# Loading one row of a weight as 85, 30 and 13 partitions instead of 128

## The chip, the cores and the metric

The kernel runs on one core of a Trainium2 chip. The metric is device time in microseconds (us); lower is better. A load is carried in packets by the 16 DMA engines that the page counts. The semaphore of a load of 128 partitions gets 16 increments in these traces; I read one increment as one engine's part landed, and the load as landed with the last of them.

A ratio below is the mean time of one kernel's fast runs over the mean of the other's in the same rounds, so it is not quite the ratio of the medians that stand beside it.

## The reference

One token (S = 1, D = 1024) goes through two branches that are added: grouped attention over a cache of 65,536 keys (4 groups of 8 heads, 128 wide), and an MLP. What matters here is how the sum ends:

```python
x = A_x
xn = _layernorm(x, axis=-1)
return x + _A_ref(xn, k_cache, v_cache, wq, wo) + _B_ref(xn, w1, w2, w3, w4)
# in _B_ref:  h2 = _gelu(_layernorm(x1) @ w3) @ w4      w4 is 3584 x 1024, bf16
```

Nearly all of the time goes into reading 170 MB of caches and weights once.

## The kernel before

All caches and weights are loaded in one stream on SyncE's queue, in the order in which it is used, through three big buffers. The weight w4 comes last, in eight pieces. Partition m holds rows 28m to 28m+27 of w4; "a row of the tile" below is one of these 28 for all 128 partitions, 2 KB a partition. A piece of n rows is n times 2 KB for each of 128 partitions.

```python
W4_PIECES = (6, 5, 6, 4, 3, 2, 1, 1)
# ... (cut)
    stream.append("w4")                      # the last item of the stream
# ... (cut)
            elif it == "w4":
                w4_v = B_w4.rearrange("(m c) n -> m c n", c=FC)
                c0 = 0
                for n in W4_PIECES:
                    go(out=t[:, c0 * D:(c0 + n) * D], in_=w4_v[:, c0:c0 + n, :].rearrange("p c n -> p (c n)"))
                    c0 += n
# ... (cut)
    def compute_w4(lo, hi):                  # two matmuls for each of the 28 rows, in order
        wt = st.tiles["w4"]
        for c in range(lo, hi):
            for j in range(2):
                row_acc(j, hT[:, c:c + 1], wt[:, D * c + 512 * j:D * c + 512 * (j + 1)])
# ... (cut)
    compute_w4(early, FC)
    out_t = ogpool.tile([64, 512], BF16, name="out_t", tag="og")
    nc.scalar.copy(out=out_t[:], in_=psB[0:64, :])
    nc.scalar.dma_start(out=out[0, 0, :].rearrange("(j n) -> j n", j=2), in_=...)   # cut
```

## Time and profile before

| | before |
|---|---|
| time, median of 3 runs (us) | 401.73 (401.62 to 401.75) |
| span of the profiled run (us) | 399.7 |
| TensorE / VectorE busy | 57% / 52% |
| DMA: share of 16 engines, rate | 98.7%, 425 GB/s |
| last w4 piece landed (us) | 394.90 to 396.90, by engine |

Three lines of the page of before: all DMA packets, then the queue of the load stream (packets, MB, share of 16 engines' span) and the queue of instruction fetches.

```profile
DMA packets 4575, 170.01 MB, mean 425 GB/s; under 512 B 467, under 2 KB 469, under 8 KB 982
...
q1 hardware_dynamic: 4560, 169.87, 98.7%
q8 instruction: 8, 0.13, 0.1%
...
```

The stream keeps the DMA engines busy for 98.7% of the span, so the kernel is bound by DMA. The eight packets of queue 8 are fetches of instructions, 16 KB each.

The chain of waits of before, its last stretch (start us, us, what):

```profile
337.53 41.96 DMA big<-in_A_v_cache_dram
...
379.51 17.39 DMA big<-in_B_w_dram
...
396.94 0.40 PE psB L221 x2
...
397.36 0.58 ACT out_t L485
```

The V load hands over to the w4 load, w4 lands at 396.90 us, and behind it are only two matmuls and the cast. The store follows. What moves the last landing moves the end.

SyncE's line of the timeline of before (start, us, what): all eight pieces are issued, the last after a wait of 14.5 us for a semaphore that the V load still used (its last increment came at 379.49 us; the last piece counts on the same one).

```profile
361.80 18.04 SPq L183 DMA_DIRECT2D big<-in_B_w_dram  x8
```

The trace also lists each increment of a load's semaphore. The sixteen of the last piece of before, in us:

```
394.90 394.96 394.96 394.99 395.06 395.11 395.26 | 396.06 | 396.51 396.54 396.55 396.60 396.66 396.76 396.81 396.90
```

Seven engines are early, one is in the middle and eight are late. The landings of the earlier loads show why. After each of the eight instruction fetches (0.94 to 1.10 us a packet, at 43.3, 106.2, 156.8, 200.3, 255.9, 297.1, 336.1 and 383.4 us) one more engine is late, by about 1.6 us, and stays so to the end; after a smaller fetch (8 KB, at 113.4 us) one more is late by about 1.1 us, the one in the middle. So each fetch went through another engine, by these counts. The engines do not catch up: a 2 KB packet takes 84 ns (median; 96 at most), early or late.

### The profile page before, as it was taken

How to read it: one execution, taken by the hardware profiler on the slowest of the kernel's cores; microseconds unless marked ns; L12 is line 12 of the kernel's file. 1: busy time of each engine (PE TensorE's matmuls, PEld its weight loads, DVE VectorE, ACT ScalarE, POOL GpSimd, SP SyncE). 2: the span in 40 equal slices, each digit the busy share in tenths (PEclk: the TensorE clock that was granted, in tenths of full speed). 3: DMA queues.
4: the chain of work that ended last, by engine and by line, in shares of the span. 5: the costliest groups of instructions: out<-in, count | busy, mean ns of one | idle time of the engine just before them, and what ended most of it. 6: DMA issues, size and time to landing. Idle time of an engine off the chain costs nothing.

```text
span 399.7 us, 2547 instructions
## 1 busy us (share of the span) xinstructions
PE 229.8 (57%) x1348; PEld 44.8 (11%) x854; DVE 209.0 (52%) x154; ACT 27.3 (7%) x35; POOL 5.4 (1%) x28
## 2 busy tenths in 40 slices
PE   0561960591579247832964296429453936494985
PEld 0210000000200110010101000201010002010241
DVE  0610010975196559644953795269349931985040
ACT  1001010003000200020002000200100020002000
POOL 2000000000000000000000000000000000000000
PEclk9996895697769587968895679679976986597999
DMA  9998999999999999999999999999999999999995
GB/s 420 420 448 384 436 485 439 426 420 420 415 427 426 446 472 421 426 420 426 433 428 466 439 420 426 415 446 426 446 448 426 420 426 402 430 469 426 397 421 227
DMA packets 4575, 170.01 MB, mean 425 GB/s; under 512 B 467, under 2 KB 469, under 8 KB 982
## 3 DMA queue, kind: packets, MB, share of 16 engines
q1 hardware_dynamic: 4560, 169.87, 98.7%
q8 instruction: 8, 0.13, 0.1%
q14 instruction: 1, 0.01, 0.0%
q10 hardware_dynamic: 6, 0.00, 0.0%
HBM read 169.87 MB, written 0.00 MB: 425 GB/s over the span
## 4 chain that ended last, share of the span: by engine, by line
DMA 52%; DVE 26%; PE 16%; ACT 3%; another core or an unknown queue 2%; issue 1%; DVEq 0%; ACTq 0%
DMA big<-in_A_k_cache_dram 31%; DVE big L357 19%; DMA big<-in_A_v_cache_dram 10%; PE sc L362 8%; PE oacc L412 6%; DMA big<-in_A_wq_dram 5%; DMA big<-in_B_w_dram 4%; DVE p_sb L383 3%; DVE mx L367 3%; ACT p_sb L380 3%; PE psq L287 1%; PE pm_mx L369 0%; DVE m L371 0%; PE pm_mx L376 0%
## 5 line engine op out<-in xcount | busy, mean ns | idle before, releaser
L362 PE MATMUL sc<-big,qdiag 128*128 128x512 bf16 x512 | 129.0, 413 | 66.8 <-DVE big L357 61.2
L357 DVE STREAM_TRANSPOSE big<-big 128x4096 f32<-128x4096 f32 x32 | 139.4, 4412 | 50.5 <-DMA big<-in_A_k_cache_dram 50.5
L412 PE MATMUL oacc<-big,p_sb 128*32 128x512 bf16 x512 | 43.0, 509 | 34.5 <-DVE p_sb L383 34.5
L367 DVE TENSOR_REDUCE mx<-sc 128x1 f32<-128x2048 f32 x8 | 18.3, 2292 | 29.8 <-PE sc L362 29.8
L362 PEld LDWEIGHTS <-qdiag 128*128 128x128 bf16 x128 | 13.2, 103 | 178.1 <-issue 145.8
L380 ACT ACTIVATE p_sb<-sc,nball 128x2048 bf16<-128x2048 f32 x8 | 15.7, 1967 | 220.6 <-DVE nball L378 220.6
L383 DVE STREAM_TRANSPOSE p_sb<-p_sb 128x2048 bf16<-128x2048 bf16 x8 | 18.5, 2312 | 18.0 <-ACT p_sb L380 18.0
L412 PEld LDWEIGHTS <-p_sb 128*32 128x32 bf16 x512 | 17.2, 124 | 57.4 <-DVE p_sb L383 35.1
L287 PE MATMUL psh<-big,ln_rep_b 128*32 128x512 bf16 (+1 forms) x64 | 12.4, 943 | 8.3 <-DMA big<-in_B_w_dram 8.3
L451 PE MATMUL o_acc<-big,oT 128*1 128x512 bf16 x48 | 12.0, 415 | 2.4 <-ACT p_sb L380 2.4
L369 PE MATMUL pm_mx<-ident_f,mx 128*1 128x128 f32 x8 | 2.4, 296 | 19.1 <-DVE mx L367 19.1
L326 DVE STREAM_TRANSPOSE h_row<-h_row 128x896 bf16<-128x896 bf16 x1 | 1.1, 1111 | 21.4 <-ACT h_row L325 21.4
L421 DVE SCALAR_TENSOR_TENSOR og<-oacc,wb,og 128x512 f32<-128x512 f32 x4 | 3.0, 746 | 16.2 <-PE oacc L412 16.2
L221 PE MATMUL psB<-big,hT 128*1 128x512 bf16 x56 | 7.4, 378 | 2.2 <-DMA big<-in_B_w_dram 2.1
L457 DVE COPY o_rows<-o_acc 1x1024 f32<-1x1024 f32 x1 | 1.2, 1212 | 12.8 <-PE oacc L412 12.8
L235 PE MATMUL pm_ln<-ln_rowsum_a,ones_f 128*128 128x1 f32 x2 | 0.6, 348 | 12.6 <-DVE ln_rowsum_a L233 12.6
L311 POOL COPY qdiag<-qx 32x32 bf16<-32x32 bf16 x16 | 3.3, 204 | 279.4 <-PE sc L362 250.3
L433 PE MATMUL pm_e<-ol,sel8big 128*128 128x129 f32 x8 | 2.3, 370 | 8.2 <-DVE ol L432 8.2
L226 DVE STREAM_TRANSPOSE x_t<-x_row 32x256 bf16<-32x256 bf16 x4 | 2.5, 616 | 8.2 <-DMA x_row<-in_A_x_dram 8.1
L287 PE MATMUL psq<-big,ln_rep_a 128*32 128x512 bf16 x64 | 5.6, 527 | 1.2 <-DMA big<-in_A_wq_dram 1.2
L376 PE MATMUL pm_mx<-ident_f,rep 1*128 1x1 f32 x8 | 1.8, 228 | 5.0 <-DVE rep L373 5.0
L299 DVE CAST q_row<-psq 128x512 bf16<-128x512 f32 x1 | 0.7, 692 | 7.5 <-PE psq L287 7.5
(95 smaller groups left out, 72.4 us busy)
## 6 DMA issues: line engine op xcount, KB each, us to landing
big<-in_A_wo_dram SPq DMA_DIRECT2D x1, 8192.0 KB, 37.2
big<-in_B_w_dram SPq DMA_DIRECT2D x1, 7168.0 KB, 38.2
big<-in_B_w_dram SPq DMA_DIRECT2D x2, 2048.0 KB, 46.4
big<-in_B_w_dram SPq DMA_DIRECT2D x2, 1536.0 KB, 27.3
big<-in_B_w_dram SPq DMA_DIRECT2D x1, 1280.0 KB, 24.1
big<-in_B_w_dram SPq DMA_DIRECT2D x1, 1024.0 KB
big<-in_B_w_dram SPq DMA_DIRECT2D x1, 768.0 KB, 30.8
big<-in_B_w_dram SPq DMA_DIRECT2D x1, 512.0 KB, 31.5
```

The source lines that it names most:

```text
L221: nc.tensor.matmul(psB[32 * j:32 * j + lhsT.shape[1], :], lhsT=lhsT, rhs=rhs, start=start, stop=False, tile_position=(0, 32 * j), skip_gro ...
L226: nc.vector.transpose(out=x_t[32 * a:32 * a + 32].rearrange("p c j -> p (c j)"), in_=x_row[:, 256 * a:256 * (a + 1)].rearrange("p (i c) -> ...
L287: nc.tensor.matmul(acc[32 * q:32 * q + 32, i, 0:n], lhsT=rep[:, c, :], rhs=cols(c, i, q), start=(c == 0), stop=(c == DC - 1), tile_positio ...
L311: nc.gpsimd.tensor_copy(out=qdiag[at, LEAD:].rearrange("p (x c) -> p x c", x=4)[:, :, 32 * a:32 * a + 8], in_=qx[at, :, 8 * g:8 * g + 8])
L357: nc.vector.transpose(out=words, in_=words)
L362: nc.tensor.matmul(sc[:, e, :], lhsT=qdiag[:, c0:c0 + P], rhs=cols[:, s, e, :, b2, :, r], start=(s == 0 and b2 == 0 and r == 0), stop=(s = ...
L367: nc.vector.reduce_max(out=mx[:], in_=sc[:].rearrange("p e n -> p (e n)"), axis=AX.X)
L380: nc.scalar.activation(out=p_sb[:], in_=sc[:], func=ACTF.Exp, bias=nball[:, b:b + 1], scale=SCALE, accum_out=group["lall"][:, b:b + 1])
L383: nc.vector.transpose(out=flat, in_=flat)
L412: nc.tensor.matmul(oacc[32 * q:32 * (q + 1), :], lhsT=pT[:, e, 32 * t:32 * (t + 1)], rhs=vt[:, :, e, t, :], start=(e == 0 and t < 4), stop ...
L421: nc.vector.scalar_tensor_tensor(out=og[:], in0=oacc[:], scalar=wb[:, 1:2], in1=og[:], op0=ALU.mult, op1=ALU.add)
L451: nc.tensor.matmul(tail["rows"][0:1, h2, :], lhsT=oT[g][:, j:j + 1], rhs=wt[:, g, j, 512 * h2:512 * (h2 + 1)], start=(g == 0 and j == 0), ...
```

## The change

The intent is to even this out: one row of the tile is not loaded over 128 partitions, 8 for each engine, but as 85, 30 and 13 partitions. The semaphores of these three loads get 5, 15 and 13 increments from DMA engines, instead of 16. If each load is dealt evenly, one of the five engines of the 85 partitions carries 17 to 20 rows, any other at most 3. The five are meant to be early engines, which take work from the late ones; that they are early was assumed.

```diff
-W4_PIECES = (6, 5, 6, 4, 3, 2, 1, 1)
+W4_PIECES = (6, 5, 6, 3, 1, 3, 2, 1, 1)
+W4_SHARED = 4
+SHARES = (85, 30, 13)
...
-                for n in W4_PIECES:
+                for i, n in enumerate(W4_PIECES):
+                    if i == W4_SHARED:
+                        p0 = 0
+                        for k in SHARES:
+                            go(out=t[p0:p0 + k, c0 * D:(c0 + n) * D],
+                               in_=w4_v[p0:p0 + k, c0:c0 + n, :].rearrange("p c n -> p (c n)"))
+                            p0 += k
+                        c0 += n
+                        continue
```

## The prediction

> What bounds the kernel. DMA. The page's queue table has the load queue's packets busy for 98.7% of 16 engines' span, 425 GB/s; TensorE is busy 57%, VectorE 52%. In the chain of waits the V load ends at 379.49 us, then the w4 load runs 17.39 us to 396.90, then two matmuls (0.40), the cast (0.58) and the store. So the landing of the last w4 piece sets the end.
>
> By the trace's DMA packet and landing records this piece lands unevenly: seven of sixteen engines at 394.90 to 395.26 us, one at 396.06, eight at 396.51 to 396.90. The lag is older: eight 16 KB instruction fetches (queue 8, about 1.06 us each) went each through one engine and left it about 1.7 us behind for good. [...] A 2 KB packet takes 80 ns from start to start; late engines do not speed up when the early ones are done.
>
> What the change does. [...] Before, each engine carried 8 rows of this row of w4. [...] The bytes are the same. Three more DMA issues (about 0.43 us each) on SyncE wait for recycled semaphores; the last waits for the third piece (landed 389.97) and starts 1.2 us later, some 2 us before the queues run dry: hidden, by estimate.
>
> How much is critical. If an engine's own rate is the only limit, the late group ends 0.4 us earlier (396.5), the early five at 394.65+0.5+0.96=396.1: 401.3. [...] One engine here moves 65,536 B in 2.414 us, 27.1 GB/s[...]. [...] No line of this trace tells which limit holds. [...]predict no gain: 401.9 us, range 401.2 to 403.2. Chances: faster by over 2% 0.005, within 2% 0.98, slower by over 2% 0.015.
>
> What would show it. Last w4 landing at 396.5 with a narrower spread if only engine rates count; 396.9 or later, with the 85-partition load's 2 KB packets longer than 84 ns[...]. Matmuls, cast and store behind it unchanged, everything before 379 us too. SyncE issues the last piece at about 390 us.
>
> What would make it wrong. [...] A last issue so late that engines idle. Instruction fetches that move.

The sum weighed two branches. If only an engine's own rate counts, five engines, supposed early and with 12 rows more each (0.96 us at 80 ns a row), end at 396.1 us and the late ones with 5 rows fewer (0.4 us) at 396.5 us, which gave 401.3 us. In the other branch, to which 60% were given, rows that other engines carry collide where they are written, and nothing is gained. Together they came to 401.9 us. One of the risks: that the five engines are not all early, put at up to 1 us.

## More of the kernel before

Stretches of the end of before. The columns are the stretch, its length, the busy time and count of PE, PEld, DVE, ACT and POOL, the granted TensorE clock, the busy share of the 16 DMA engines, and GB/s:

```profile
core 0: us, PE busy (x) PEld busy (x) DVE busy (x) ACT busy (x) POOL busy (x), PEclk, DMA share, GB/s
387.00:389.00 2.00, 1.98 (x18) 0.95 (x20) 0.94 (x4) 0.00 (x0) 0.00 (x0) 1.00 0.99 416
389.70:390.70 1.00, 1.00 (x14) 0.37 (x10) 0.00 (x0) 0.00 (x0) 0.00 (x0) 1.00 1.03 428
390.70:391.70 1.00, 1.00 (x12) 0.41 (x9) 0.00 (x0) 0.00 (x0) 0.00 (x0) 1.00 0.99 410
391.70:392.70 1.00, 0.42 (x6) 0.09 (x3) 0.00 (x0) 0.00 (x0) 0.00 (x0) 1.00 0.99 404
392.70:393.70 1.00, 0.83 (x8) 0.26 (x5) 0.00 (x0) 0.00 (x0) 0.00 (x0) 1.00 0.99 395
393.70:394.70 1.00, 0.32 (x4) 0.17 (x5) 0.00 (x0) 0.00 (x0) 0.00 (x0) 1.00 0.93 361
```

The DMA share stays near 1.00 and the rate near 400 to 430 GB/s until engines run out of work.

## The result, and the profile after

| | before | after |
|---|---|---|
| time, median of 6 runs (us) | 401.62 (401.40 to 401.75) | 403.27 (403.03 to 403.55) |
| span of the profiled run (us) | 399.7 | 401.3 |
| last w4 piece landed (us) | 394.90 to 396.90 | 396.01 to 398.28 |

The ratio is 1.0041 (95% interval 1.0028 to 1.0054): slower by 1.65 us, outside the predicted range by 0.07 us and far from its centre.

The same lines of the page of after:

```profile
DMA packets 4736, 170.01 MB, mean 424 GB/s; under 512 B 500, under 2 KB 502, under 8 KB 1271
...
q1 hardware_dynamic: 4721, 169.87, 98.7%
q8 instruction: 8, 0.13, 0.1%
...
```

The bytes and the share of the queue are the same, with 161 packets more. The page as a whole hides what happened.

The chain of waits of after, its last stretch:

```profile
338.16 41.31 DMA big<-in_A_v_cache_dram
...
379.49 16.24 DMA big<-in_B_w_dram
...
395.77 3.17 PE psB L231 x14
...
398.96 0.58 ACT out_t L495
```

The chain names a piece that landed at 395.73 us and fourteen matmuls that ran without a gap after it. The last two of these still had to wait for the last piece, and that landed at 398.28 us, 1.38 us later than before. (Why there was no gap is told at the end of this section.)

SyncE's lines of the timeline of after: three loads of the shared row at 363.97 us, and the last four pieces from 379.49 on.

```profile
362.17 1.75 SPq L193 DMA_DIRECT2D big<-in_B_w_dram  x4
363.97 1.16 SPq L188 DMA_DIRECT2D big<-in_B_w_dram  x3
379.49 10.90 SPq L193 DMA_DIRECT2D big<-in_B_w_dram  x4
```

The last issue is at 390.06 us, as predicted, and its data land 6 to 8 us later, behind the queue. Issue is not what is late.

The stretches of after:

```profile
core 0: us, PE busy (x) PEld busy (x) DVE busy (x) ACT busy (x) POOL busy (x), PEclk, DMA share, GB/s
387.00:389.00 2.00, 1.74 (x16) 0.73 (x14) 1.38 (x5) 0.00 (x0) 0.00 (x0) 1.00 1.00 418
389.70:390.70 1.00, 1.00 (x12) 0.43 (x10) 0.00 (x0) 0.00 (x0) 0.00 (x0) 1.00 1.01 260
390.70:391.70 1.00, 1.00 (x14) 0.37 (x10) 0.00 (x0) 0.00 (x0) 0.00 (x0) 1.00 1.08 272
391.70:392.70 1.00, 0.79 (x8) 0.23 (x5) 0.00 (x0) 0.00 (x0) 0.00 (x0) 1.00 1.01 268
392.70:393.70 1.00, 0.65 (x6) 0.17 (x5) 0.00 (x0) 0.00 (x0) 0.00 (x0) 1.00 0.98 324
393.70:394.70 1.00, 0.54 (x4) 0.12 (x3) 0.00 (x0) 0.00 (x0) 0.00 (x0) 1.00 0.98 393
```

This is the main reading. The early engines reach the shared row at 389.2 us, and from 389.7 us the 16 DMA engines are as busy as before (1.01, 1.08, 1.01), but they move 260, 272 and 268 GB/s instead of 428, 410 and 404. Busy share counts the time that packets are under way, so packets that take longer look busy.

The packet records say the same by packet. Between 389.9 and 392.9 us all 96 packets of 6 KB took 321 ns or more (median 359; in e1_pieces below, with the same pieces, 239.5), and all 89 of 2 KB took 98 ns or more (median 133; 84 there). No packet was spared, not even the 6 KB ones, which belong to loads of 128 partitions. The window is chosen to hold the stall: the first packets of the shared row, from 389.18 us, still took 84 to 92 ns; the slowing sets in for 2 KB and 6 KB packets alike between 389.6 and 389.8 us, and it is over at 393.8 us.

The landings by engine of the pieces that matter, in us:

```
85 partitions (5 engines):   391.80 392.06 392.12 392.15 | 393.77
last piece (16 engines):     396.01 396.03 396.14 | 397.07 397.13 397.14 397.20 397.22 397.25 397.30 397.33 397.43 397.52 397.65 397.72 | 398.28
```

Two things stand out. Thirteen of the sixteen engines end later than the latest engine of before (396.90), twelve of them by 0.2 to 0.8 us, although eleven engines were given fewer rows (at most 3 of the shared row, not 8, if the loads are dealt evenly). And one engine ends 0.56 us after all the others; by its lag it is one of the five with 17 rows or more, whose part of the 85 partitions landed 1.6 us after the other four. Only three of the seven early engines of before are still early in the last piece, so four of the five chosen engines were early ones, and the fifth was not. (The records carry no engine numbers; this is inferred from the counts.)

A small third part shows in the profiled run: from the last landing to the end of the cast it took 1.26 us (398.28 to 399.54) instead of 1.04 (396.90 to 397.94). Stretches of after at its end:

```profile
396.00:397.00 1.00, 1.00 (x6) 0.26 (x3) 0.00 (x0) 0.00 (x0) 0.00 (x0) 0.50 0.69 260
397.00:398.00 1.00, 1.00 (x8) 0.44 (x6) 0.00 (x0) 0.00 (x0) 0.00 (x0) 0.50 0.08 31
398.00:398.90 0.90, 0.90 (x6) 0.08 (x1) 0.00 (x0) 0.00 (x0) 0.00 (x0) 0.50 0.00 0
```

The granted TensorE clock was 0.50 there, and the matmuls fell behind and ran back to back. In the profiled run this is 0.22 of the 1.6 us by which the span grew; the other runs of after have no trace, so what it is worth in them is not known. It is not the main cause: the clock was 1.00 in the same place in the profiles of e2_even and e3_four below, which lose 1.44 and 1.55 us.

### The profile page after: what moved, and what is told of

The parts are those of the page before. It is cut to its first block, busy times and chain, and to the rows that moved or that the text cites. A ratio compares the mean times of both kernels' runs of the same rounds, so it can differ in the third digit from the quotient of the medians.

```text
span 401.3 us, 2551 instructions
## 1 busy us (share of the span) xinstructions
PE 233.7 (58%) x1348; PEld 44.6 (11%) x854; DVE 209.0 (52%) x154; ACT 27.3 (7%) x35; POOL 5.3 (1%) x28
## 4 chain that ended last, share of the span: by engine, by line
DMA 51%; DVE 26%; PE 17%; ACT 3%; another core or an unknown queue 2%; issue 1%; DVEq 0%; ACTq 0%
DMA big<-in_A_k_cache_dram 31%; DVE big L367 18%; DMA big<-in_A_v_cache_dram 10%; PE sc L372 8%; PE oacc L422 6%; DMA big<-in_A_wq_dram 5%; DMA big<-in_B_w_dram 4%; DVE p_sb L393 3%; DVE mx L377 3%; ACT p_sb L390 3%; PE psq L297 2%; PE psB L231 1%; DVE m L381 0%; PE pm_mx L379 0%
## 5 line engine op out<-in xcount | busy, mean ns | idle before, releaser
L422 PE MATMUL oacc<-big,p_sb 128*32 128x512 bf16 x512 | 45.4, 526 | 34.5 <-DVE p_sb L393 34.5
L231 PE MATMUL psB<-big,hT 128*1 128x512 bf16 x56 | 8.5, 438 | 2.1 <-DMA big<-in_B_w_dram 2.1
```

Source lines behind the costliest of these rows:

```text
L231: nc.tensor.matmul(psB[32 * j:32 * j + lhsT.shape[1], :], lhsT=lhsT, rhs=rhs, start=start, stop=False, tile_position=(0, 32 * j), skip_gro ...
L422: nc.tensor.matmul(oacc[32 * q:32 * (q + 1), :], lhsT=pT[:, e, 32 * t:32 * (t + 1)], rhs=vt[:, :, e, t, :], start=(e == 0 and t < 4), stop ...
```

## The experiments

Three theories were to be told apart. C: rows that are handed to other engines collide where they are written, and this slows the loads. U: the uneven counts are the loss, because an engine that already lags got more rows. P: the extra pieces, small packets and recycled semaphores cost time. Later a fourth came up, H: the rows are read from HBM in a worse order. Times that stand without their condition in the expectations of e7_comb and e8_alone2 are those for theory C. Counts of engines are known from increments: 16 for 128 partitions, 5 for 85, 4 for 68, 3 for 51, 15 for 30, 13 for 13. No count was taken for 80, 64 and 48 partitions, multiples of 16 as 128 is; 16 engines for these is my estimate from the counts above. Ten kernels ran in three jobs, on three chips; all gave correct results. The medians of before in the three jobs were 401.64, 401.65 and 401.57 us.

### e1_pieces: the pieces without the sharing

```diff
 # before.py
-W4_PIECES = (6, 5, 6, 4, 3, 2, 1, 1)
+W4_PIECES = (6, 5, 6, 3, 1, 3, 2, 1, 1)
```

> The pieces of the change (6, 5, 6, 3, 1, 3, 2, 1, 1), but every one a load of 128 partitions: no sharing. Theory C[...] and theory U (the five engines carry too many rows): neither is present, so the time of before, 401.5 to 401.8 us, last w4 landing about 396.9 us. Rival P (one more piece, smaller packets, waits of SyncE for recycled semaphores): most of the loss stays, 402.5 to 403.3 us.

Measured: 401.64 us (401.62 to 401.68), ratio 1.0001 (0.9986 to 1.0016). Two stretches of it:

```profile
389.70:390.70 1.00, 1.00 (x12) 0.43 (x10) 0.00 (x0) 0.00 (x0) 0.00 (x0) 1.00 1.07 432
...
391.70:392.70 1.00, 1.00 (x12) 0.38 (x10) 0.00 (x0) 0.00 (x0) 0.00 (x0) 1.00 1.03 418
```

The rate is that of before, and the last piece landed at 396.76 us. P falls: neither the ninth piece nor its issue costs anything that can be seen. (The change has two issues more than this kernel; e7_comb, with one more, shows no loss clear of the noise either.)

### e2_even: other rows, equal counts by estimate

```diff
 # after.py
-SHARES = (85, 30, 13)
+SHARES = (80, 48)
```

> The shared row as loads of 80 and 48 partitions[...]. Theory C: slow packets (2 KB well over 84 ns) around 390 to 393 us on all engines, last landing 397.3 to 398.3 us, 402.2 to 403.2 us in all. Theory U (uneven counts are the whole loss): as before, 401.5 to 401.9 us.

Measured: 403.08 us (402.75 to 403.25), ratio 1.0037 (1.0020 to 1.0054); last landing 398.04 us. Three stretches of it:

```profile
389.70:390.70 1.00, 1.00 (x12) 0.44 (x10) 0.00 (x0) 0.00 (x0) 0.00 (x0) 1.00 1.05 274
390.70:391.70 1.00, 1.00 (x12) 0.35 (x7) 0.00 (x0) 0.00 (x0) 0.00 (x0) 1.00 1.03 336
391.70:392.70 1.00, 0.11 (x2) 0.00 (x0) 0.00 (x0) 0.00 (x0) 0.00 (x0) 1.00 1.08 244
```

By the estimate above each engine has 5 + 3 = 8 rows of this row of the tile, as before, and most of the loss is there. If so, U as the whole cause falls. The same stall is seen: full DMA share at 244 to 336 GB/s.

### e3_four: four engines instead of five

```diff
 # after.py
-SHARES = (85, 30, 13)
+SHARES = (68, 60)
```

> 68 and 60 partitions[...]. Under both theories the load on the writers is about that of the change. [...]the 68-partition load has no straggler and the end comes near that of the other engines, 402.5 to 402.9 us; [...]403.2 to 403.7 us.

The first time is for the case that the straggler of the change (393.77 us against 391.80 to 392.15) is not among the four engines of the 68 partitions, the second for the case that it is.

Measured: 403.19 us (403.07 to 404.37), ratio 1.0046 (1.0031 to 1.0061). The 68 partitions landed at 391.90, 391.91, 392.38 and 393.71 us, and four engines instead of three were early in the last piece. So the straggler is still among the chosen ones (393.71 us).

### e4_alone: single loads by themselves

```diff
 # before.py, after the last matmul
+    for n in (128, 85, 80, 64, 30, 16, 13, 5, 128):
+        nc.sync.dma_start(out=w4_t[0:n, 0:8 * D], in_=w4_all[0:n, 0:8, :].rearrange("p c n -> p (c n)"))
```

Each load overwrites the one before it, so each waits until that one has landed: its first packet starts 0.94 to 1.36 us after the last landing of the one before (seven gaps).

> The kernel before, and after its last matmul nine loads of w4, one at a time, 16 KB a partition (605 ns a packet in the main stream), of 128, 85, 80, 64, 30, 16, 13, 5 and 128 partitions. If only an engine's own rate counts, the packets of each take rows per engine times 0.6 us: 4.8, 10.3, 3.0, 2.4, 1.2, 0.6, 0.6, 0.6, 4.8. [...] Total time about 450 us; results correct.

Measured (one look; first packet to last landing): 85 partitions 17.43 us, 80: 6.88, 64: 6.35, 30: 3.61, 16: 3.17, 13: 3.01, 5: 3.02, the last 128: 6.34. The first 128 overlapped with the stream and is left out. A load of 64 partitions takes as long as one of 128 (6.35 and 6.34 us) with half the rows; if both have 16 engines (an estimate), 4 rows an engine against 8, engine rates alone do not explain that. A load of 5 takes about as long as one of 16; with one row an engine in both (an estimate, as 13 partitions got 13 increments), this fits either theory. (e9_alone3 below settles it.) These times hold the landing too, and the expectation was of the packets alone. The 85 partitions need 17.43 us where 17 rows at 0.61 us, the time of a 16 KB packet in the stream, would be 10.4: the five engines are slowed even alone. In the small loads it is the landing that is late (16 partitions: packets done after 2.06 us, landed after 3.17).

### e5_dose: three rows of the tile shared instead of one

```diff
 # after.py
-W4_SHARED = 4
+W4_SHARED = 3
-SHARES = (85, 30, 13)
+SHARES = (80, 48)
```

> As e2_even (80 and 48 partitions[...]), but the piece that is shared is the one of three rows of w4 instead of one. Theory C, loss by collisions[...]: about three times the 1.44 us of e2_even, 404.8 to 406.2 us. Rival (a cost per load that is not of 128 partitions, whatever its size): as e2_even, 402.9 to 403.4 us.

Measured: 404.89 us (404.75 to 405.04), ratio 1.0080 (1.0065 to 1.0095). Two stretches of it:

```profile
389.70:390.70 1.00, 1.00 (x12) 0.35 (x10) 0.55 (x2) 0.00 (x0) 0.00 (x0) 0.97 0.85 176
...
391.70:392.70 1.00, 1.00 (x12) 0.35 (x10) 0.00 (x0) 0.00 (x0) 0.00 (x0) 1.00 1.08 188
```

The loss grows with the bytes: 3.24 us (404.89 less 401.65) against 1.44 (403.08 less 401.64), 2.25 times for three times the bytes. It is no fixed cost of a load with few partitions. It also is not quite proportional.

### e6_halves and e7_comb: neighbours against every other partition

```diff
 # after.py: e6_halves
-SHARES = (85, 30, 13)
+SHARES = (64, 64)
```

```diff
 # after.py: e7_comb
-SHARES = (85, 30, 13)
+SHARES = (0, 1)
-                            go(out=t[p0:p0 + k, c0 * D:(c0 + n) * D],
-                               in_=w4_v[p0:p0 + k, c0:c0 + n, :].rearrange("p c n -> p (c n)"))
-                            p0 += k
+                            go(out=t[k::2, c0 * D:(c0 + n) * D],
+                               in_=w4_v[k::2, c0:c0 + n, :].rearrange("p c n -> p (c n)"))
```

> The shared row as partitions 0 to 63 and 64 to 127[...]. Theory C: [...]slower than before by 0.6 to 1.6 us, 402.2 to 403.3 us. Theory U (uneven counts alone): 401.5 to 401.9 us.

> The same two loads of 64 partitions[...], but of the even and of the odd partitions[...]. [...]nearer to before, 401.6 to 402.4 us[...]. If it comes from loads of fewer than 128 partitions as such: as e6_halves.

Measured: e6_halves 402.78 us (402.61 to 403.08), ratio 1.0028 (1.0011 to 1.0044); e7_comb 401.85 us (401.67 to 401.88), ratio 1.0003 (0.9988 to 1.0018). Stretches of e6_halves, then of e7_comb:

```profile
389.70:390.70 1.00, 1.00 (x12) 0.37 (x10) 0.00 (x0) 0.00 (x0) 0.00 (x0) 1.00 1.09 303
390.70:391.70 1.00, 1.00 (x12) 0.44 (x10) 0.00 (x0) 0.00 (x0) 0.00 (x0) 1.00 1.00 328
391.70:392.70 1.00, 0.91 (x10) 0.26 (x5) 0.00 (x0) 0.00 (x0) 0.00 (x0) 1.00 1.12 291
```

```profile
389.70:390.70 1.00, 1.00 (x12) 0.44 (x10) 0.00 (x0) 0.00 (x0) 0.00 (x0) 1.00 1.07 430
390.70:391.70 1.00, 0.98 (x12) 0.30 (x8) 0.00 (x0) 0.00 (x0) 0.00 (x0) 1.00 1.01 404
391.70:392.70 1.00, 1.00 (x8) 0.22 (x8) 0.00 (x0) 0.00 (x0) 0.00 (x0) 1.00 1.02 414
```

The two differ in nothing but which 64 partitions make a load. With neighbours the rate falls to 291 to 328 GB/s; with every other partition it stays at 404 to 430 GB/s, the packets stay at 84 ns for 2 KB, and the loss is gone within the noise. So it is not the number of partitions of a load that costs, but where its partitions lie.

### e8_alone2: neighbours against spread partitions, alone

```diff
 # before.py, after the last matmul
+    for n, step in ((16, 1), (128, 8), (32, 1), (128, 4), (64, 1), (128, 2), (128, 1)):
+        nc.sync.dma_start(out=w4_t[0:n:step, 0:8 * D], in_=w4_all[0:n:step, 0:8, :].rearrange("p c n -> p (c n)"))
```

> The kernel before, then single loads alone, 16 KB a partition: 16 neighbouring partitions, 16 partitions 8 apart, 32 neighbours, 32 that are 4 apart, 64 neighbours, 64 that are 2 apart, 128. [...] first packet to last landing about 3.2 and 1.9, 3.2 and 1.9, 6.3 and 3.9, 6.3 us. If only engine rates count: within each pair the same, about 1.9, 1.9, 3.9 us and less.

Measured (one look): 16 partitions 8 apart 2.08 us; 32 neighbours 3.70, 32 that are 4 apart 2.45; 64 neighbours 6.28, 64 that are 2 apart 3.83; 128: 6.49. The first load overlapped with the stream and says nothing; 3.17 us of e4_alone stands for it. In each pair the spread partitions take less. From 32 to 64 neighbours the time nearly doubles (3.70 to 6.28 us), and from 64 to 128 it stays (6.49): the second 32 partitions behave as if they shared a limit with the first 32, the other 64 as if they had their own. The loads of 32 took 0.5 us longer than I had expected.

### e9_alone3: destination or source

In e6, e7 and e8 the partitions written and the rows read change together, so H was still open: 64 neighbours also read neighbouring stretches of w4. Here the two are set apart.

```diff
 # before.py, after the last matmul
+    for n, ds, ss in ((128, 1, 1), (64, 1, 1), (64, 1, 2), (64, 2, 1), (64, 2, 2), (16, 1, 8), (16, 8, 1), (5, 1, 1), (5, 4, 4)):
+        nc.sync.dma_start(out=w4_t[0:n * ds:ds, 20 * D:28 * D],
+                          in_=w4_all[0:n * ss:ss, 20:28, :].rearrange("p c n -> p (c n)"))
```

> The kernel before, then single loads alone, 16 KB a partition, after the last matmul (the tile is dead by then, so the results stay correct): 128 rows as a start; 64 rows with destination / source neighbouring or 2 apart in all four combinations; 16 rows to 16 neighbours from rows 8 apart and the reverse; 5 rows to 5 neighbours, and to 5 partitions that are 4 apart. [...]the destination alone decides: 6.3, 6.3 (neighbours) and 3.9, 3.9 us (2 apart), 3.2 and 2.1 us for 16 rows, 3.0 and about 1.6 to 1.9 us for 5 rows. If it sits in reading the rows (rival H), the source alone decides: 6.3, 3.9, 6.3, 3.9.

Measured (one look), as stretches from the first packet of each load to its last landing; the second column is its duration, the last its rate. In order: 64 rows to neighbours from neighbours, to neighbours from every other, to every other from neighbours, to every other from every other; 16 rows to neighbours, 16 rows to partitions 8 apart; 5 rows to neighbours, 5 rows to partitions 4 apart.

```profile
405.58:412.07 6.49, 0.00 (x0) 0.00 (x0) 0.00 (x0) 0.00 (x0) 0.00 (x0) 0.50 0.74 162
413.34:419.35 6.01, 0.00 (x0) 0.00 (x0) 0.00 (x0) 0.00 (x0) 0.00 (x0) 0.50 0.80 174
420.64:424.46 3.82, 0.00 (x0) 0.00 (x0) 0.00 (x0) 0.00 (x0) 0.00 (x0) 0.50 0.76 275
425.75:429.51 3.76, 0.00 (x0) 0.00 (x0) 0.00 (x0) 0.00 (x0) 0.00 (x0) 0.50 0.76 275
430.49:433.58 3.09, 0.00 (x0) 0.00 (x0) 0.00 (x0) 0.00 (x0) 0.00 (x0) 0.50 0.41 85
434.92:436.87 1.95, 0.00 (x0) 0.00 (x0) 0.00 (x0) 0.00 (x0) 0.00 (x0) 0.50 0.45 134
437.78:440.52 2.74, 0.00 (x0) 0.00 (x0) 0.00 (x0) 0.00 (x0) 0.00 (x0) 0.50 0.12 30
442.10:443.50 1.40, 0.00 (x0) 0.00 (x0) 0.00 (x0) 0.00 (x0) 0.00 (x0) 0.50 0.21 59
```

The destination decides: 6.49 and 6.01 us to neighbours, 3.82 and 3.76 us to every other partition, whatever is read. H falls for loads by themselves; in the stream no run sets the two apart. The last two lines are the plainest: five rows need 2.74 us to neighbours, and 1.40 us to partitions 4 apart (from rows 4 apart; I had expected 1.6 to 1.9).

### e10_three: three engines with 17 rows or more

```diff
 # after.py
-SHARES = (85, 30, 13)
+SHARES = (51, 77)
```

> 51 and 77 partitions[...]. Theory C alone[...]: as e2_even to e3_four, 402.9 to 403.4 us. If the load of the most loaded engine adds to it: [...]403.5 to 404.2 us[...]; [...]the time falls to 402.5 to 403.0 us.

The last time, 402.5 to 403.0 us, is for the case that the engine that lags by 1.2 us is not among the three; the one before it is for the case that it is.

Measured: 402.77 us (402.69 to 402.94), ratio 1.0030 (1.0013 to 1.0047). The 51 partitions landed at 392.27, 392.47 and 392.49 us: no straggler, with as many rows an engine of this load as in the change (51 on 3 and 85 on 5, 17 each if dealt evenly). The chain of waits of e10_three, its end:

```profile
386.01 11.87 DMA big<-in_B_w_dram
...
397.92 0.40 PE psB L231 x2
```

The last landing is at 397.88 us. By these landings the straggler is among the five of the change and the four of e3_four, and not among the three here (taken as one engine, an inference). Being rid of it is worth 0.50 us (403.27 less 402.77, from different jobs with the same time of before), which fits the 0.56 us by which it trailed in the change. (By the last landings alone it is 0.40 us, 398.28 less 397.88; the rest may be the slower clock at the end of the profile of after, and the rows are also dealt otherwise.) Three engines with 17 rows or more each cost no more than e2_even, whose counts are even by the estimate above (402.77 against 403.08 us), so uneven counts of early engines do not set the end.

## Why the prediction was wrong, point by point

- The bound was right. DMA sets the end and the last w4 landing moves it. What comes before is as it was: the V load ahead of the tail landed at 379.47 us, against 379.49.
- The number of engines was right: the semaphores of the three loads got 5, 15 and 13 increments from DMA engines, and one entry each within 0.6 us of the issue (364.47, 364.89, 365.30 us), of which the trace does not tell the writer. Which engines they are, no run here shows.
- The hidden issues were right: the last at 390.06 us, and neither e1_pieces nor e7_comb shows a loss clear of the noise. Matmuls and cast behind the last landing were not quite unchanged: 1.26 us instead of 1.04 in the profiled run.
- The branch on which I put 60%, collisions where the rows are written, was right. What I had said would show it came: a last landing after 396.9 (398.28 us) and 2 KB packets longer than 84 ns (133 in the median). e6_halves, e7_comb and e9_alone3 show the cause: with the same number of partitions and bytes, the partitions that are written decide (6.49 and 6.01 us to neighbours, 3.82 and 3.76 us to every other partition). So the other branch, a gain of 0.4 us if only engine rates count, is not what the runs show: 64 neighbours take about as long as 128 partitions (6.28 and 6.49 us in e8_alone2).
- The step that failed is the cost of the collisions, in its reach and in its size. My text had only the engines slowed that carry the shared row, and weighed against the gain of the other branch this became "no gain: 401.9 us". Its size was an estimate that did not rest on this case. The runs showed a stall of all sixteen engines instead (6 KB packets of 359 ns in the median where e1_pieces has 239.5), and by the estimate of engine counts it comes without any engine having more rows than before (e2_even). It cost 1.1 to 1.4 us (e6_halves 1.13, e10_three 1.20, e2_even 1.44), and on top of it came 0.2 to 0.5 us for a second term that I had listed as what could go wrong and left out of the sum.
- That second term is the premise that the five chosen engines are all early. Before's trace did not show it. By e3_four and e10_three one chosen engine was not early, and by its lag it is the one in the middle, 1.2 us behind (an inference). It got 9 to 12 rows more, if the loads are dealt evenly, and became the last of all. This could have been asked of the trace: it shows seven early engines, and nothing in it said that the five chosen ones were among them.

What stays open: why the stall takes hold of all engines. Every 6 KB packet slowed at the same time, by 1.3 times or more, 1.5 in the median (321 ns or more, 359 in the median, against 239.5), and no run here shows where the packets wait.

## What to carry to other kernels

Before moving work between DMA engines, ask what else sets the time of each byte: here it was the partition that is written (64 rows alone: 6.49 us to neighbours, 3.82 us to every other partition), and handing rows to other engines did not relieve it (403.27 us against 401.62). Split a load into every other partition rather than into halves of neighbours (e7_comb 401.85 us against e6_halves 402.78). And a DMA share near 1.00 is no proof of full rate: look at GB/s in the same stretch (1.01 at 260 GB/s in after, 1.03 at 428 in before).
